# A two-headed sequence-mixer kernel (FFT convolution and diagonal state space): convolution rows split by parity, and its outer stages in pieces of the array

## The chip, the cores and the metric

The kernel runs on one core of one Trainium2 chip. The metric is device microseconds of one execution; lower is better. All tensors are bf16, sums are made in f32.

## The reference, cut to what matters

Two independent heads work on 2048 rows of 1024 channels and are written side by side.

```python
def _A_ref(q, k, v, shift_k, ssm_k, ssm_D):       # head A: (1, 2048, 1024)
    k_shift = zeros_like(k)
    for t in range(4):                            # a causal filter of 4 taps for each channel
        k_shift = k_shift + k_pad[:, t:t + S, :] * shift_k[:, 3 - t]
    kv = k_shift * v
    y = irfft2(rfft2(kv padded to 2S) * rfft2(ssm_k padded to 2S))[:S]   # a long convolution over rows
    return q * (y + kv * ssm_D)

def _B_ref(x, Lambda, Bmat, Cmat, log_dt, Dskip): # head B: 1024 complex states
    Lam_bar = exp(dt * Lam); Bu = x @ (((Lam_bar - 1) / Lam)[:, None] * Bmat).T
    for t in range(L): h = Lam_bar * h + Bu[t]    # a recurrence over the rows
    return 2 * (hseq @ Cmat.T).real + x * Dskip

return concatenate([a, b], axis=-1)               # (1, 2048, 2048)
```

## The kernel before, in words

Head A's convolution is a Fourier transform of length 4096 taken apart into two steps (128 by 32), in matrix products. Its rows are numbered n·16 + r, with n in 0..127 on the partitions and r in 0..15.

- **kv stage.** `kp` loads two rows r of k into the ring `kring`, `vp` two rows of v; `kvm`, `kva`, `kvb`, `kvc` (DVE) make kv. `am` (PE, L610) multiplies by the first Fourier matrix `F1t`, for two groups u of frequencies; `ae` (ACT) evicts, `ast` stores to the DRAM tile `Ys_kv`.
- **filter stage.** `hl` loads the filter `ssm_k` into `hk`, `hT` transposes on PE, `hm` (L643) is the same first step, `he` evicts, `hst` stores to `Ys_h`.
- **second step**, in 16 groups `gq`. `lh` and `lk` load 512 KiB each from `Ys_h` and `Ys_kv`; `sh`, `sk` (PE, L676) multiply by a table `wts`, in quarters of the array (64 by 64); `she`, `ske` (ACT) evict. For the complex product, `sw` copies the filter's result onto the neighbouring partitions by four DMAs of 128 KiB, so that real and imaginary parts are exchanged, and `pr` (DVE, L704) multiplies both. `sa` (PE, L717) goes back, `sae` evicts, `vst` stores to `Vs`.
- **last step.** `vl` loads from `Vs`, `a3` (PE, L744) multiplies by the last matrix `Gt`, `a3e` evicts, `qm` multiplies by q (loaded by `qp`), `ost` stores to the output.

Head B: `bl` loads and `bT` (PE, L458) transposes the matrix B, `bc` evicts it to `BT`; `cx` and `x` load C and x by DMA transposes. In 16 chunks of 128 rows: `U` (PE, L492), `ue`, `r1`..`r4` and `sc` (DVE; `sc` is a scan over the recurrence), `y` (PE, L546), `ye`, `yst`.

Everything is written out by hand: a long table, `ORDER`, gives the sequence of all these steps, which is the order on every engine, and behind each colon the buffers that the step takes. Transfers go on the queue of SP or POOL: `spd` on SP unless the word has `@G`, `gpd` on POOL unless it has `@S`. On each queue they are issued in this order, and a transfer that waits for a buffer or for data holds back those behind it.

In DRAM the rows of one transfer of 128 partitions are evenly spaced: `kr = k.rearrange("(n s) d -> n s d", s=NR)` for k, v, q and the output, and, for the 512 KiB loads and stores of the second step,

```python
    Ys_kv = tc.dram_tile([2, NR, P, D], BF16, name="Ys_kv")
    Ysv = lambda Y, gq: Y.rearrange("u r (e g) d -> (u r e) g d", g=32)[:, 2 * gq:2 * gq + 2, :]
```

Of the kernel before, what the change touches and what calls it, by code (L numbers as in the profile page):

```python
# [14 lines left out]
ALU = mybir.AluOpType  # L15
# [12 lines left out]
def a_constants():  # L28
    n1 = np.arange(64)[:, None]; k1 = np.arange(64)[None, :]
    ang = 2 * np.pi * n1 * (k1 + 0.5) / N1  # L30
    F = np.stack([np.cos(ang), -np.sin(ang)], axis=1).reshape(64, 2, 2, 32)
    F1 = np.zeros((64, 2, 2, 2, 2, 32))
    G1 = np.zeros((2, 2, 32, 2, 64, 2))
    for h in range(2):
        F1[:, h, :, h] = np.transpose(F, (0, 2, 1, 3))
        G1[h, :, :, :, :, h] = np.transpose(F, (1, 3, 2, 0)) * (2 / NFFT)
# [5 lines left out]
    WF = np.zeros((2, N2, 2, 32, 3, N2))  # L42
    t = lambda a: np.transpose(a, (0, 2, 1, 3))
    WF[:, :, 0, :, 0, :] = t(c_); WF[:, :, 1, :, 0, :] = t(s_)
    WF[:, :, 0, :, 1, :] = t(-s_); WF[:, :, 1, :, 1, :] = t(c_)
    WF[:, :, :, :, 2, :] = WF[:, :, :, :, 0, :]
    WI = np.zeros((2, 2, N2, 16, 2, 2, N2, 2))
    for gi in range(2):
        for ui in range(2):
            for gq in range(16):  # L50
                cc = np.transpose(c_[ui, 2 * gq + gi], (1, 0)); ss = np.transpose(s_[ui, 2 * gq + gi], (1, 0))
                o = WI[gi, :, :, gq, ui]
                o[0, :, 0, :, 0] = cc; o[0, :, 0, :, 1] = ss
                o[1, :, 0, :, 0] = -cc; o[1, :, 0, :, 1] = -ss
                for cp in range(2):
                    o[cp, :, 1, :, 0] = -ss; o[cp, :, 1, :, 1] = cc
    W = np.concatenate([WF.reshape(128, NWP, 4 * 96), WI.reshape(128, NWP, 2 * 256)], axis=2)
# [5 lines left out]
NA = 11  # L63
# [15 lines left out]
ue.2.1 ae.4.0:b13 hm.0.2.0:d2 am.4.1:d1 z2 ast.4.0 am.0.0:d0 U.2.3.0:p0 hst.0.1.1 ae.4.1:b4 U.1.1.1 he.0.2.0:b7 ast.4.1@S sc.0 U.2.3.1 ue.1.1
hst.0.2.0@S hm.0.2.1:d1 cx.7.1 ue.2.3 am.5.1:d2 ae.0.0:b6 hT.0.4:p1 cx.2.1 am.2.0:d0 hc.0.4:b10 ast.0.0 U.1.0.0:p0 ae.2.0:b3 hT.0.7:p1 cx.4.0 kva.8  # L80
U.1.0.1 ue.1.0 hT.0.5:p0 hc.0.7:b0 hl.5:a9 kvb.8:a4 hl.4:a2 U.2.0.0:p1 hc.0.5:b13 ast.2.0@S hl.7:a3 r3.0:m0 U.1.3.0:p0 he.0.2.1:b8 am.1.0:d0 hst.0.2.1
hm.0.5.0:d1 U.1.3.1 cm.0:a7 kvc.8 U.2.0.1 ue.1.3 he.0.5.0:b11 r4.0 U.4.0.0:p0 ue.2.0 hm.0.4.0:d1 r1.1:m0 U.4.0.1 he.0.4.0:b5 U.4.2.0:p1 ue.4.0:a5
hst.0.4.0@S ae.5.1:b6 hm.0.7.1:d1 r2.1 U.4.2.1 ae.1.0:b4 ast.5.1 U.4.1.0:p0 hl.6@G:a10 r1.2:m0 he.0.7.1:b7 ast.1.0@S hst.0.5.0 am.8.1:d2 ue.4.2
U.4.1.1 hm.0.5.1:d0 sc.1 am.5.0:d1 he.0.5.1:b8 U.4.3.0:p1 ue.4.1 am.2.1:d0 ae.5.0:b3 y.0.0.0:p0 ae.2.1:b13 hm.0.4.1:d1 hm.0.7.0:d0 ast.2.1@S U.4.3.1
x.3:b6 he.0.7.0:b10 r2.2:a0 am.8.0:d0 ae.8.1:b5 hst.0.7.0 y.0.0.1 r3.1:m0 hst.0.5.1 ue.4.3 ast.8.1@S ast.5.0@S y.0.0.2 ae.8.0:b0 vp.3:a8 y.0.1.0:p1
ast.8.0 cm.1 hst.0.7.1 r4.1 am.3.0:d2 y.0.1.1 ae.3.0:b4 r1.4:m0 y.0.0.3 ast.3.0 ye.0.0:b11 hT.1.4:p0 y.0.1.2 sc.2 hc.1.4:b13 he.0.4.1:b10 hT.1.3:p0
hm.1.4.1:d0 am.9.0:d2 hc.1.3:b9 hst.0.4.1@S ae.9.0:b8 hT.1.5:p0 am.9.1:d1 y.0.1.3 he.1.4.1:b5 r2.4:a5 am.3.1:d2 ye.0.1 hst.1.4.1 hm.1.3.1:d0
y.1.1.0:p1 he.1.3.1:b0 kvm.6:m0 hc.1.5:b3 y.1.1.1 hst.1.3.1@S ae.3.1:b7 hT.1.7:p0 y.1.1.2 ae.9.1:b4 hm.1.4.0:d0 hm.1.5.1:d2 hc.1.7:b10 ast.9.1 y.1.1.3
kp.6 kva.6 hT.1.6:p0 ast.9.0@S ye.1.1:b5 kp.5 hm.1.7.0:d1 hc.1.6:b13 yst.0@S y.1.0.0:p1 ast.3.1@S he.1.5.1:b0 hT.1.1:p0 cm.2:a4 kvb.6:a1 y.1.0.1
hst.1.5.1 hc.1.1:b4 lw.1@G:w0 hm.1.6.0:d2 r3.2:m0 y.1.0.2 he.1.6.0:b2 y.1.0.3 he.1.4.0:b8 hst.1.6.0@S hT.1.0:p0 r4.2 ye.1.0 hst.1.4.0 hm.1.6.1:d2  # L90
# [56 lines left out]
def full_kernel(ctx, tc, A_q, A_k, A_v, A_shift_k, A_ssm_k, A_ssm_D, B_x, B_Lre, B_Lim, B_Bre, B_Bim,  # L147
# [96 lines left out]
    def k8(name, shape):  # L244
        return rtile(ap_pool("a2"), "e", name, shape)
# [578 lines left out]
```

## Time and profile before

| | |
|---|---|
| median of three runs | 377.3 us (377.26, 377.30, 383.09) |
| the profiled execution | span 378.5 us |
| busy: PE, DVE, ACT, POOL | 346.6, 324.6, 264.2, 81.3 us |
| moved by DMA | 100.06 MB, mean 264 GB/s over the 16 DMA engines |

Times are microseconds unless marked ns. PE is the matrix engine, PEld its weight loads, DVE the vector engine, ACT the scalar engine, POOL GpSimd, SP the queue engine; a q behind a name is its sequencer. A row of a group gives line, engine, operation, what it writes and reads, and the count; then busy time and mean ns of one; then the idle time of the engine just before, and what ended it. In a row of a DMA queue stand packets, MB and the share of the 16 engines' time that these packets took.

### The profile page before, as it was taken

What the parts mean: (1) busy time and instruction counts of PE and PEld (TensorE: products, weight loads), DVE (VectorE), ACT (ScalarE), POOL (GpSimd) and SP (SyncE); (2) the same over time, 40 slices, a digit from 0 to 9 for tenths busy, and PEclk for the clock granted to TensorE, in tenths of its full rate; (3) what the DMA queues carried; (4) which work ended last, traced back from release to release, by engine and by line L of the source; (5) the groups of instructions that cost most, each with busy time, mean ns of one, the idle gap of its engine ahead of it and who ended that gap; (6) DMA issues with size and microseconds to landing.
All of it is one profiled execution on the core that took longest, in us unless ns stands there. A gap on an engine that the chain in (4) does not pass through costs nothing.

```text
span 378.5 us, 8748 instructions
## 1 busy us (share of the span) xinstructions
PE 346.6 (92%) x3661; PEld 225.6 (60%) x3661; DVE 324.6 (86%) x229; ACT 264.2 (70%) x341; POOL 81.3 (21%) x150
## 2 busy tenths in 40 slices
PE   4548889899899999999999999989999999999995
PEld 3226678785455578855444757367867664467442
DVE  6989599999999997999997797576899999993972
ACT  4978798877778886952785879778869771346433
POOL 7300023022112521214200325330210202211021
PEclk9999999999999999999999999999999999999999
DMA  6999999997578999999999897999989539877995
GB/s 231 317 338 216 265 272 286 296 314 235 200 243 270 247 313 287 281 272 268 190 275 312 258 324 234 220 267 221 284 236 312 175 125 325 306 229 255 350 319 206
DMA packets 67418, 100.06 MB, mean 264 GB/s; under 512 B 38435, under 2 KB 42147, under 8 KB 67380
## 3 DMA queue, kind: packets, MB, share of 16 engines
q1 hardware_dynamic: 54660, 56.32, 54.8%
q0 software_dynamic: 12720, 43.19, 36.8%
q8 instruction: 28, 0.46, 0.5%
q14 instruction: 10, 0.08, 0.1%
HBM read 49.16 MB, written 33.55 MB: 219 GB/s over the span
## 4 chain that ended last, share of the span: by engine, by line
PE 56%; DMA 15%; issue 13%; ACT 7%; SPq 4%; POOL 2%; DVE 1%; POOLq 0%; ACTq 0%; DVEq 0%
PE ps_u L492 22%; PE ps_y L546 16%; PE ps_a L744 4%; DMA wts<-a_c_W 4%; SPq L483 4%; DMA Ys_kv<-ysb 3%; PE ps_a L643 3%; DMA l2k<-Ys_kv 3%; DMA ld<-in_B_B_re_dram 3%; PE ps_a L717 3%; PE ps_a L610 3%; DMA hab<-hab 2%; PE ps_a L676 2%; PE ps_t L630 2%; ACT ysb L615 2%
## 5 line engine op out<-in xcount | busy, mean ns | idle before, releaser
L492 PEld LDWEIGHTS <-BT 128*128 128x128 bf16 x2048 | 119.3, 98 | 22.6 <-issue 11.7
L492 PE MATMUL ps_u<-xT,BT 128*128 128x128 bf16 x2048 | 127.7, 219 | 2.4 <-ACT u L497 1.2
L546 PE MATMUL ps_y<-CT,h 128*128 128x512 bf16 x512 | 127.7, 379 | 0.0
L546 PEld LDWEIGHTS <-h 128*128 128x128 bf16 x512 | 44.6, 98 | 48.0 <-issue 6.1
L523 DVE TENSOR_TENSOR_SCAN h<-rtab,h 128x2080 bf16<-128x2080 f32 x16 | 71.8, 4488 | 0.2
L497 ACT CAST u<-ps_u 128x512 bf16<-128x512 f32 x64 | 38.2, 603 | 27.0 <-PE ps_u L492 19.1
L506 DVE TENSOR_TENSOR mt<-u,Z 128x4096 bf16<-128x4096 bf16 x16 | 36.7, 2291 | 15.8 <-ACT u L497 15.4
L704 DVE TENSOR_TENSOR hab<-x,hab 128x4096 bf16<-128x4096 bf16 x16 | 36.5, 2286 | 15.2 <-DMA hab<-hab 10.5
L556 ACT CAST yo<-ps_y 128x512 bf16<-128x512 f32 x32 | 19.1, 596 | 28.0 <-PE ps_y L546 24.4
L650 ACT CAST ysbh<-ps_a 128x1024 bf16<-128x1024 f32 x32 | 32.3, 1033 | 8.8 <-PE ps_a L643 7.5
L691 ACT CAST x<-ps_a 128x1024 bf16<-128x1024 f32 x32 | 31.9, 1026 | 8.8 <-PE ps_a L676 5.9
L506 DVE TENSOR_TENSOR mt<-h,Z 128x4096 bf16<-128x4096 bf16 x16 | 36.7, 2292 | 0.5
L724 ACT CAST vsb<-ps_a 128x1024 bf16<-128x1024 f32 x32 | 31.7, 1027 | 6.5 <-PE ps_a L717 6.0
L583 DVE TENSOR_TENSOR mt<-kring,wbc 128x2048 bf16<-128x2048 bf16 (+3 forms) x14 | 35.8, 2592 | 0.4 <-ACT wbc L473 0.2
L615 ACT CAST ysb<-ps_a 128x1024 bf16<-128x1024 f32 x32 | 32.3, 1043 | 2.7 <-issue 1.6
L685 ACT CAST hab<-ps_a 128x1024 bf16<-128x1024 f32 x32 | 32.2, 1030 | 2.1 <-PE ps_a L676 1.9
L551 PE MATMUL ps_y<-Dd,xT 128*128 128x128 bf16 x128 | 28.0, 219 | 0.0
L749 ACT CAST ot<-ps_a 128x1024 bf16<-128x1024 f32 x16 | 15.7, 1018 | 14.1 <-PE ps_a L744 14.1
L169 POOL DMA_DIRECT2D Ys_h<-ysbh x20 | 14.3, 716 | 43.3 <-ACT ysbh L650 43.3
L168 POOL DMA_DIRECT2D hab<-hab x32 | 15.6, 494 | 32.1 <-ACT hab L685 18.3
L458 PE MATMUL ps_t<-ident,ld 128*128 128x128 bf16 x128 | 13.9, 285 | 9.1 <-DMA ld<-in_B_B_re_dram 4.4
L643 PE MATMUL ps_a<-hT,F1t 128*128 128x512 bf16 x64 | 20.6, 402 | 0.8 <-ACT ysbh L650 0.6
(116 smaller groups left out, 381.8 us busy)
## 6 DMA issues: line engine op xcount, KB each, us to landing
Ys_h<-ysbh POOLq DMA_DIRECT2D x20, 256.0 KB, 5.5
l2h<-Ys_h SPq DMA_DIRECT2D x9, 512.0 KB, 9.7
Vs<-vsb SPq DMA_DIRECT2D x9, 512.0 KB, 4.3
vv<-Vs SPq DMA_DIRECT2D x9, 512.0 KB, 5.2
Ys_kv<-ysb POOLq DMA_DIRECT2D x17, 256.0 KB, 6.2
l2k<-Ys_kv SPq DMA_DIRECT2D x8, 512.0 KB, 3.9
hab<-hab SPq DMA_DIRECT2D x32, 128.0 KB, 5.4
l2k<-Ys_kv POOLq DMA_DIRECT2D x8, 512.0 KB, 7.8
```

Source lines behind the costliest of these rows:

```text
L492: nc.tensor.matmul(pu[:, w, jl, :], BT[:, 2 * jp + jl, w, d, :], xT[:, d, :], start=(d == 0), stop=(d == ND - 1))
L497: nc.scalar.copy(u[:, :, 2 * jp:2 * jp + 2, :], st["pu", i, jp][:])
L506: nc.vector.tensor_mul(m, s_, w_)
L523: nc.vector.tensor_tensor_scan(gf, rtab[:].rearrange("p a j t -> p (a j t)"), gf, 0.0, ALU.mult, ALU.add)
L546: nc.tensor.matmul(py[:], h[:, 1 - w, j, 2:TP], CT[:, j, w, dh * 512:(dh + 1) * 512], start=(j == 0 and w == 0), stop=(j == NJ - 1 and w = ...
L583: nc.vector.tensor_mul(m[:, :, j0:j0 + n, :], a_, wbc[:, j0:j0 + n, :].unsqueeze(1).to_broadcast([P, 2, n, DV]))
L615: nc.scalar.copy(st["ysb", r, u][:], st["pa", r, u][:].rearrange("p e d -> p (e d)"))
L643: nc.tensor.matmul(pd[:, e, :], F1t[:, u, :], st["hT", f, rp][:, e, :], start=True, stop=not sk)
L650: nc.scalar.copy(st["yh", f, rp, u][:], st["pa", f, rp, u][:])
L685: nc.scalar.copy(hab[:, a, :, e * 512:(e + 1) * 512], st["ps", key, gq, e][:])
L691: nc.scalar.copy(x16[:, :, e * 512:(e + 1) * 512], st["ps", "k", gq, e][:])
L704: nc.vector.tensor_mul(hab, x16.unsqueeze(1).to_broadcast([P, 2, 2 * D]), hab)
```

## The change

It rewrites head A's data layout and half of B's load. Its parts:

1. **Rows by parity.** Row numbers are read as (n, h, s): h is the parity of the block of 16 rows. The partition is now h·64 + n. A load of k, v, q and a store of head A's output takes both parities in one transfer, whose DRAM side has the counts [2][64][2048] (output [2][64][1024]) in place of [128][2048].
2. **Outer stages in array pieces.** `am` works on parities and frequency groups in quarters of the array (64 by 64); `a3` has 64 output rows for each parity, in halves. The DRAM tiles are `[NR, 2, P, D]`, one store `ast` for both halves, and the second step's loads and stores have the counts [4][32][2048] in DRAM.
3. **Real and imaginary on one partition.** `sh`, `sk` and `sa` run in eighths of the array (64 by 32, and 32 by 64), with real and imaginary parts beside each other in the free dimension. The 64 copies `sw` and `pr` go; `p1` multiplies with the parts read in the other order, `p0` without.
4. **Filter rows in C's space.** `hk` is two tiles of 16 KiB per partition, one after the other in the place that the second half of C (`ct`) takes later. So the second filter load, on POOL, waits for the first half's transposes `hT`, and the loads of C's second half, on SP from `cx.7.1` on, wait for the second half's.
5. **Half of B by DMA transpose**: `bx` loads 8 of the 16 tiles straight into `BT`; their `bl`, `bT`, `bc` go.
6. Small: `dd` is one DVE product, not 8 ACT copies; `sc` is two scans of 1040 in place of one of 2080, on one table; the order and the buffers are all new.

| transfer | KiB | on SP, on POOL before | on SP, on POOL now | DRAM counts now |
|---|---|---|---|---|
| k (r ≥ 0) | 512 | 3, 5 | 8, 0 | 2, 64, 2048 |
| v | 512 | 4, 4 | 6, 2 | 2, 64, 2048 |
| q | 512 | 6, 2 | 4, 4 | 2, 64, 2048 |
| output of A | 256 | 9, 7 | 10, 6 | 2, 64, 1024 |
| l2h | 512 | 9, 7 | 10, 6 | 4, 32, 2048 |
| l2k | 512 | 8, 8 | 12, 4 | 4, 32, 2048 |
| Vs | 512 | 9, 7 | 11, 5 | 4, 32, 2048 |
| hab copies | 128 | 32, 32 | none | |

```diff
-    Ys_kv = tc.dram_tile([2, NR, P, D], BF16, name="Ys_kv")
+    Ys_kv = tc.dram_tile([NR, 2, P, D], BF16, name="Ys_kv")
...
-    kr = k.rearrange("(n s) d -> n s d", s=NR)
-    oar = out_a.rearrange("(n s) d -> n s d", s=NR)
+    rows = lambda a: a.rearrange("(n h s) d -> h n s d", s=NR, h=2)
+    two = lambda a, r: a.rearrange("(n h s) d -> h n (s d)", s=NR, h=2)[:, :, 2 * r * D:(2 * r + 2) * D]
+    flat = lambda t_: t_.rearrange("p s d -> p (s d)")
+    oar = rows(out_a)
...
-    Ysv = lambda Y, gq: Y.rearrange("u r (e g) d -> (u r e) g d", g=32)[:, 2 * gq:2 * gq + 2, :]
+    Ysv = lambda Y, gq: Y.rearrange("r h (e g) d -> e (r h) (g d)", g=32)[:, :, 2 * gq * D:(2 * gq + 2) * D]
...
-            spd(t_, kr[:, 2 * r:2 * r + 2, DX:])
+            spd(flat(t_), two(k, r))
...
-        spd(st["v", r][:], vr[:, 2 * r:2 * r + 2, :])
+        spd(flat(st["v", r][:]), two(v, r))
...
-            nc.tensor.matmul(pd[:, e, :], F1t[:, u, :], kvt(r)[:, r % 2, e * 512:(e + 1) * 512], start=True, stop=True)
+            for h in range(2):
+                for u in range(2):
+                    nc.tensor.matmul(st["pa", r][e][64 * u:64 * u + 64, h, :], F1t[64 * h:64 * h + 64, 2, 64 * u:64 * u + 64],
+                                     kvt(r)[64 * h:64 * h + 64, r % 2, e * 512:(e + 1) * 512], start=True, stop=True,
+                                     tile_position=(64 * h, 64 * u))
...
-    def sw(gq):
-        hab = st["hab", gq]
-        for b in range(4):
-            o = b ^ 1
-            spd(hab[32 * b:32 * b + 32, 1, :, :], hab[32 * o:32 * o + 32, 0, :, :])
-        nc.vector.tensor_mul(hab, x16.unsqueeze(1).to_broadcast([P, 2, 2 * D]), hab)
+    def p1(gq):
+        nc.vector.tensor_mul(st["pq", gq][:], st["sk", gq][:], st["sh", gq][:, :, ::-1, :])
+    def p0(gq):
+        nc.vector.tensor_mul(st["sh", gq][:], st["sk", gq][:], st["sh", gq][:])
...
+        for ri in range(2):
+            for j in range(4):
+                for u in range(2):
+                    nc.tensor.matmul(pd[u][32 * j:32 * j + 32, ri, :], wt[up, b0:b0 + 32],
+                                     st[nm, gq][up, j // 2, (j % 2) * 512:(j % 2 + 1) * 512], start=True, stop=True,
+                                     tile_position=(64 * u, 32 * j))
...
-            for u in range(2):
-                nc.tensor.matmul(pd[:, e, :], Gt[:, u, :], st["vv", r][:, u, e * 512:(e + 1) * 512], start=(u == 0), stop=(u == 1))
+            for h in range(2):
+                nc.tensor.matmul(pd[64 * h:64 * h + 64, e, :], Gt[:], st["vv", r][:, h, e * 512:(e + 1) * 512], start=True, stop=True,
+                                 tile_position=(0, 64 * h))
...
-        spd(st["qt", r][:], qr[:, 2 * r:2 * r + 2, :])
+        spd(flat(st["qt", r][:]), two(q, r))
...
-    E["ost"] = lambda r: gpd(oar[:, r, :], st["ot", r][:])
+    E["ost"] = lambda r: gpd(oar[:, :, r, :], st["ot", r][:])
```

Three places on SP's queue show how the transfers stand. The rows give line, operation, what is written and read, and the counts of the written side. The first place is near the start, where k, the filter and the first x are loaded; before:

```order
L168 DMA hk<-in_A_ssm_k_dram 128x2048
L168 DMA ld<-in_B_B_re_dram 128x1024
L168 DMA kring<-in_A_k_dram 128x2048
L483 DMA_TRANSPOSE xT<-in_B_x_dram 128x8x128
L480 DMA_TRANSPOSE CT<-in_B_C_im_dram 128x8x128
```

and now, from the first k load with both parities:

```order
L155 DMA kring<-in_A_k_dram 128x1x2048
L155 DMA hk<-in_A_ssm_k_dram 128x2048 x4
L460 DMA_TRANSPOSE BT<-in_B_B_im_dram 128x8x128
L155 DMA ld<-in_B_B_re_dram 128x1024
L460 DMA_TRANSPOSE BT<-in_B_B_re_dram 128x8x128
L155 DMA kring<-in_A_k_dram 128x1x2048
L463 DMA_TRANSPOSE ct<-in_B_C_re_dram 128x8x128
L155 DMA v<-in_A_v_dram 128x1x2048
```

All eight k loads are now on SP, with four filter loads and the B transposes between them; the written side of a k load stays 128 partitions, in three counts like its source. The second place is the second step, where loads of l2h and l2k, stores of Vs and, before, the copies within `hab` alternate; before:

```order
L168 DMA l2k<-Ys_kv 128x2048
L168 DMA hab<-hab 32x2048 x4
L169 DMA out_dram<-yo 128x1024
L483 DMA_TRANSPOSE xT<-in_B_x_dram 128x8x128
L168 DMA l2h<-Ys_h 128x2048
L483 DMA_TRANSPOSE xT<-in_B_x_dram 128x8x128
L169 DMA Vs<-vsb 128x2048
```

and now:

```order
L155 DMA l2k<-Ys_kv 128x1x2048 x3
L155 DMA l2h<-Ys_h 128x1x2048
L468 DMA_TRANSPOSE xT<-in_B_x_dram 128x8x128
L156 DMA Vs<-vsb 4x32x2048
L155 DMA l2k<-Ys_kv 128x1x2048 x2
L156 DMA Vs<-vsb 4x32x2048
```

The copies are gone, more of the loads follow each other on SP, and the store to Vs has the counts 4, 32, 2048. The third place is SP's end, with the last loads of q and Vs and the stores of both heads (`ot` is head A's, `yo` head B's); before:

```order
L168 DMA qt<-in_A_q_dram 128x2048
L169 DMA out_dram<-ot 128x1024 x4
L169 DMA out_dram<-yo 128x1024
L169 DMA out_dram<-ot 128x1024
L169 DMA out_dram<-yo 128x1024
```

and now:

```order
L155 DMA qt<-in_A_q_dram 128x1x2048
L155 DMA vv<-Vs 128x2x1024 x3
L156 DMA out_dram<-ot 2x64x1024 x3
L156 DMA out_dram<-yo 128x1024
L156 DMA out_dram<-ot 2x64x1024 x6
L156 DMA out_dram<-yo 128x1024
L156 DMA out_dram<-ot 2x64x1024
```

The loads of q all stand ahead of the last stores, ten of head A's stores end SP's queue, and each has the counts 2, 64, 1024.

More of the change, by code (lines that the diff above doesn't have):

```diff
@@ L666, in full_kernel, with s2 @@
     E["lk"] = lambda gq: l2("l2k", Ys_kv, gq)
[L668 removed]
+    def s2(key, nm, gq):
         wt = st["w", gq // 2]
[L670 to L678 removed]
@@ new lines, in full_kernel, with spe @@
+    E["sh"] = lambda gq: s2("h", "l2h", gq)
+    E["sk"] = lambda gq: s2("k", "l2k", gq)
+    def spe(key, gq, u):
+        s16 = once(("s" + key, gq), lambda: k4("s16", [P, 2, 2, 512]))
+        nc.scalar.copy(s16[:, u, :, :], st["ps", key, gq][u][:])
+    E["she"] = lambda gq, u: spe("h", gq, u)
+    E["ske"] = lambda gq, u: spe("k", gq, u)
+    def p1(gq):
+        st["pq", gq] = k4("pq", [P, 2, 2, 512])
+        nc.vector.tensor_mul(st["pq", gq][:], st["sk", gq][:], st["sh", gq][:, :, ::-1, :])
@@ new lines, in full_kernel, with sa @@
+    E["p1"] = p1
+    def p0(gq):
+        nc.vector.tensor_mul(st["sh", gq][:], st["sk", gq][:], st["sh", gq][:])
+    E["p0"] = p0
+    def sa(gq):
+        wt = st["w", gq // 2]
+        pd = [dtile("ps_a") for _ in range(2)]
+        st["ps", "v", gq] = pd
+        for t, (m, src, ri) in enumerate(((0, "sh", 0), (1, "sh", 1), (2, "pq", 0), (2, "pq", 1))):
+            for j in range(4):
+                for u in range(2):
+                    jp = slice(32 * j, 32 * j + 32)
+                    b0 = 256 + (gq % 2) * 384 + u * 192 + m * 64
+                    nc.tensor.matmul(pd[j // 2][64 * u:64 * u + 64, j % 2, :], wt[jp, b0:b0 + 64],
+                                     st[src, gq][jp, u, ri, :], start=(t == 0), stop=(t == 3),
+                                     tile_position=(32 * j, 64 * u))
```

357 lines of the change are left out of this document (154 added, 203 removed).

## The prediction

> **What bounds the kernel now.** I read the page's head first, then the slices, the chain, and the kernel by stages.
>
> ```profile
> span 378.5 us, 8748 instructions
> PE 346.6 (92%) x3661; PEld 225.6 (60%) x3661; DVE 324.6 (86%) x229; ACT 264.2 (70%) x341; POOL 81.3 (21%) x150
> ...
> PE   4548889899899999999999999989999999999995
> DMA  6999999997578999999999897999989539877995
> GB/s 231 317 338 216 265 272 286 296 314 235 200 243 270 247 313 287 281 272 268 190 275 312 258 324 234 220 267 221 284 236 312 175 125 325 306 229 255 350 319 206
> DMA packets 67418, 100.06 MB, mean 264 GB/s; under 512 B 38435, under 2 KB 42147, under 8 KB 67380
> ...
> q1 hardware_dynamic: 54660, 56.32, 54.8%
> q0 software_dynamic: 12720, 43.19, 36.8%
> ...
> PE 56%; DMA 15%; issue 13%; ACT 7%; SPq 4%; POOL 2%; DVE 1%; POOLq 0%; ACTq 0%; DVEq 0%
> 0.00:20.00 20.00, 9.48 (x55) 5.66 (x56) 16.40 (x50) 14.26 (x23) 10.56 (x25) 1.00 0.87 273
> 20.00:40.00 20.00, 13.77 (x84) 8.73 (x84) 17.79 (x21) 14.57 (x28) 1.27 (x2) 1.00 1.12 279
> ```
>
> PE is busy 92% of the span, and leads the chain with 56%. Of its idle 32 us, the first 40 us hold 40 − 9.48 − 13.77 = 16.8 us. After that PE is the bound, DVE close behind. But the second resource is as full as PE: the packets took 54.8% + 36.8% = 91.6% of the time of all 16 DMA engines. That holds because every large transfer is even over the 16; whatever puts more on a few of them makes these the bound. The profiled execution (378.5 us) is 0.3% over the median of the runs (377.3), so I make the sums against the span and give them as times.
>
> **The transfers, the term that decides.** What sets how many engines a transfer uses? Nearly all of the kernel's have 128 rows on both sides. The small parameter loads near the start do not:
>
> ```profile
> praw<-in_B_log_dt_dram SPq DMA_DIRECT2D x1, 2.0 KB
> praw<-in_B_Lambda_re_dram SPq DMA_DIRECT2D x1, 2.0 KB
> praw<-in_B_Lambda_im_dram SPq DMA_DIRECT2D x1, 2.0 KB
> praw<-in_B_Dskip_dram SPq DMA_DIRECT2D x1, 2.0 KB
> ...
> q1 hardware_dynamic: 64, 0.01, 2.2%
> ```
>
> The last row is of the window 1.6 to 3.8 us, when SP's queue moved just these four: 64 packets, 0.01 MB. Four loads of 8 rows make 32 data packets, so 32 others are completions: 8 a load, not 16. A transfer whose outer count is 8 went to 8 engines, one share and one completion each. The change gives outer counts of 2 (k, v, q, output) and 4 (l2h, l2k, Vs) on the DRAM side. If a transfer is cut along its outermost count, these go to 2 and to 4 engines.
>
> The Trainium skill says so: in "DMA: Bandwidth & Descriptors", section "Why a DMA increments its semaphore by 16 and not by 1", the engines are the largest number up to 16 that divides the outermost count of both sides, on SP's queue the lowest-numbered ones, on GpSimd's a run of neighbours from a cursor that moves on. By that, 128 against 2 gives 2 engines, always the same pair on SP. The trace agrees for 8 rows (the 64 packets); no run here shows a count that differs between the sides, or which engines serve.
>
> Whether SP's share always falls on the same pair no row tells; I take it so, since nothing in the program would move it, and keep the other case as a rival. Bytes on each engine of that pair, from the table of the change:
>
> - SP, count 2: k, v, q are 18 × 524,288 B, A's output 10 × 262,144 B: 12.06 MB, halved 6.03 MB.
> - SP, count 4: 33 × 524,288 B = 17.30 MB, a quarter 4.33 MB.
> - POOL, counts 2 and 4: 21 × 524,288 + 6 × 262,144 B = 12.58 MB; evenly spread 0.79 MB.
> - All else: 100.06 MB, less 64 copies of 131,072 B (8.39), plus 0.25 for the longer tables, is 91.92; less the three sums above it is 49.98 MB, a sixteenth 3.12 MB.
>
> Together 14.27 MB on each of two engines, against 100.06 / 16 = 6.25 MB now. Their rate:
>
> ```profile
> DMA packets 287, 0.86 MB, mean 430 GB/s; under 512 B 32, under 2 KB 32, under 8 KB 286
> ```
>
> That is the window 350 to 352 us, one of the fastest: 430 / 16 = 26.9 GB/s an engine. The best slice of the page has 350 / 16 = 21.9, the mean 264 / 16 = 16.5. The 10.36 MB of confined transfers are rows of 2 to 4 KB like that window's: 10.36 / 26.9 = 385 us. The other 3.91 MB have small packets among them; SP's queue moved 56.32 MB in 54.8% of 16 × 378.5 us, 17.0 GB/s: 230 us. Sum **615 us** in which the pair must work. Not all overlaps: two stage joins leave it waiting.
>
> ```profile
> Ys_kv<-ysb POOLq DMA_DIRECT2D x17, 256.0 KB, 6.2
> Vs<-vsb SPq DMA_DIRECT2D x9, 512.0 KB, 4.3
> vv<-Vs SPq DMA_DIRECT2D x9, 512.0 KB, 5.2
> out_dram<-ot SPq DMA_DIRECT2D x9, 256.0 KB, 5.0
> ```
>
> Between the last k and the first l2k stand a store (6.2) and about 12 us of kv work (an estimate from the DVE and ACT groups of that stage); between the last Vs and the outputs 4.3 + 5.2 us and about 2.5 of PE and ACT; at the end 5.0. That is 35 us: **650 us**. The ends: everything at 26.9 GB/s, 14.27 / 26.9 = 530 us; everything at 16.5, 865 us.
>
> What waits there: a k load that now needs 262,144 / 26.9 GB/s = 9.7 us of its pair holds `kvm`, and the transposes of B, x and C behind it on the same engines complete only with their last share; so `U` on PE waits too. The removed copies and PE work give nothing back while PE waits for loads.
>
> **The other parts**, which decide only if the transfers spread:
>
> ```profile
> L492 PE MATMUL ps_u<-xT,BT 128*128 128x128 bf16 x2048 | 127.7, 219 | 2.4 <-ACT u L497 1.2 <-ACT BT L473 0.9 <-ACT hT L635 0.3
> L458 PE MATMUL ps_t<-ident,ld 128*128 128x128 bf16 x128 | 13.9, 285 | 9.1 <-DMA ld<-in_B_B_re_dram 4.4 <-DMA ld<-in_B_B_im_dram 2.5 <-ACT BT L473 1.2
> L610 PE MATMUL ps_a<-acc,F1t 128*128 128x512 bf16 x64 | 19.0, 387 | 0.4 <-ACT ysb L615 0.2 <-ACT ysbh L650 0.2
> L676 PE MATMUL ps_a<-l2h,wts 64*64 64x512 bf16 x128 | 11.3, 387 | 3.0 <-DMA wts<-a_c_W 2.3 <-DMA l2h<-Ys_h 0.7
> L676 PE MATMUL ps_a<-l2k,wts 64*64 64x512 bf16 x128 | 10.8, 385 | 0.0
> L717 PE MATMUL ps_a<-hab,wts 64*64 64x512 bf16 x256 | 18.2, 383 | 0.8 <-DVE hab L704 0.7
> L744 PE MATMUL ps_a<-vv,Gt 128*128 128x512 bf16 x64 | 16.1, 379 | 0.0
> L473 ACT COPY BT<-ps_t 128x1024 bf16<-128x1024 bf16 x14 | 13.9, 1013 | 4.9 <-PE ps_t L458 4.9
> L704 DVE TENSOR_TENSOR hab<-x,hab 128x4096 bf16<-128x4096 bf16 x16 | 36.5, 2286 | 15.2 <-DMA hab<-hab 10.5 <-ACT x L691 4.6
> L518 DVE TENSOR_TENSOR h<-mt 128x2048 bf16<-128x2048 bf16 x16 | 19.5, 1220 | 0.3
> L523 DVE TENSOR_TENSOR_SCAN h<-rtab,h 128x2080 bf16<-128x2080 f32 x16 | 71.8, 4488 | 0.2
> ```
>
> - PE, B: 64 of 128 transposes go, half of 13.9: −7.0 us; 8 evictions of 1.013 go from ACT, under PE's work.
> - PE, `am`: 64 products at 19.0 us become 128 in quarters; at L717's 18.2 / 256 = 71 ns that is 9.1: −9.9.
> - PE, `a3`: 64 of half the array. Between half of 16.1 us (two beside each other, as the quarters run four) and all of it; I take half: −8.0.
> - PE, second step: 512 quarters at 11.3 + 10.8 + 18.2 = 40.3 us become 1024 eighths. If eight run beside each other, 40.3; if each costs what a quarter does (71 ns), 72.7; if as L492's pairs of load and product (127.7 / 2048 = 62 ns), 63.5. Ends 0 and +32; I take +10, nearer the quarters, which already ran four at once.
> - DVE: 16 products at 2.286 become 32 at 1.220: +2.5. Halving the length from 4096 to 2048 costs 2 × 1.220 − 2.286 = 0.15 us an extra instruction, so 16 more scans cost 2.4. `dd` on DVE is one product of 1024, below the 1.220 of a 2048 one. DVE ends 15.2 us of waits at L704, 10.5 of them for the copies; that is more than the added 6, and PE covers both.
> - The wait on the filter's place (part 4): behind `cx.7.1` on SP stand the other C loads and x. It waits for a transpose written just ahead of it in the table; at no more than 2 to 3 us it hides under the 16.8 us of PE's early idleness; uncovered, it adds itself.
> - The added price of issuing is none: 64 issues fewer.
>
> Sum on PE: −7.0 − 9.9 − 8.0 + 10 = −15, ends −25 and +15 (with `a3` at no gain and eighths at quarters' price).
>
> On the eighths the Trainium skill ("TensorE: Matmul & The Clock Gate", "Packing small matmuls — row/col tiling") has pieces in different places of the array start about 4 ns apart and run together; by that the step stays near 40 us and the sum is −25. The trace shows four at once, 71 ns where L744's full products take 16.1 / 64 = 252 ns; no run here shows eight.
>
> **The rivals.**
>
> 1. *The transfers spread over all 16 engines* (the cut is made on the 128 partitions, or across both counts). For it: the SBUF side still has 128; the row for 8 rows had 8 on both sides, so it can't tell. Then PE decides: 378 − 15 = **362 us**, ends 353 and 393. This is the side that is not slower; the point is the number of engines: 16 in place of 2.
> 2. *Spread, and the small pieces cost their issue*: the same with +32 and no gain at `a3`: **393 us**.
> 3. *Few engines at a time, but not the same ones each time.* Total load falls to 91.92 / 16 = 5.75 MB an engine, less than now. Single transfers last 9.7 us in place of the 4 to 6 us of the landings above; those on the way between stages show: two joins and the first k, about 5 us each: 362 + 15 = **377 us**.
> 4. *Only one of the counts confines.* With 2 spread: 4.33 MB at 26.9 and about 4.7 at 17: 435 us. With 4 spread: 6.03 and about 5.0: 518 us.
>
> **How the numbers follow.** The confined case 0.79, predicted 650 us, its own range 530 to 865; rival 4 gets 0.04, rival 1 0.11, rival 3 0.04, rival 2 0.02. The range reaches down to 430 to take in rival 4 and up to 865: about 0.81 inside. Within 2% (370 to 385 us; 2% is about what a measurement of this kernel can tell from no change) lies rival 3 and a bit of rival 1: 0.05. Faster 0.10, slower 0.85.
>
> **What would show it.** Right: landings of k, v and q rise from about 5 to well over 15 us and those of transposes with them, mean GB/s falls to about 92 MB / 650 us = 141 while the slices of DMA never show more than two or three tenths for long, PE busy near half, and the chain is DMA by most of its share. Wrong in the step on counts: landings stay near 5 us and the mean over 240 GB/s. Wrong in the rate: few engines, but a span far from 650, by waits of SP at its own queue. If the pieces of the array mislead, it is seen in the busy time of `sh`, `sk` and `sa`, against 40.3 us.

## The result, and the profile after

The changed kernel takes **702.5 us** (median of four executions, 701.4 to 704.4), the kernel before 377.3 beside it on the same chip: the ratio is 1.865, 95% interval 1.856 to 1.874. The forecast was 650, in the range 430 to 865. The executions of some of the kernels below scatter by 1 to 2% on a chip, and one of run 7 took 1936 us; each ratio and interval leaves the disturbed ones out, while the medians given take all.

The page of the kernel after, its head, slices, queues and chain; the profiled execution took 704.4 us.

```profile
span 702.4 us, 9560 instructions
PE 375.7 (53%) x4133; PEld 232.9 (33%) x4173; DVE 321.2 (46%) x258; ACT 259.0 (37%) x329; POOL 58.8 (8%) x92
...
PE   4762048045477498995859575656068600392300
...
DMA  8998964299979959955543337122355224464111
GB/s 212 156 113 64 90 157 180 99 90 150 134 143 264 105 201 88 160 188 96 70 127 110 128 131 215 54 118 117 118 172 182 78 95 140 155 216 136 72 62 53
DMA packets 85881, 92.03 MB, mean 131 GB/s; under 512 B 58671, under 2 KB 64319, under 8 KB 85840
...
q1 hardware_dynamic: 62768, 58.76, 50.0%
q0 software_dynamic: 23072, 32.67, 15.0%
...
DMA 43%; PE 20%; SPq 20%; issue 7%; ACT 4%; DVE 1%; POOL 0%; POOLq 0%; ACTq 0%
```

No engine is the bound any more: PE is busy 53%, and the two queues' packets took 65% of the engines' time where it was 91.6%. Bytes fell by 8%, but the rate halved from 264 to 131 GB/s. Read the two DMA rows together at the right end. In the last slices one tenth of the 16 engines moves 62 and 53 GB/s: two engines at the 26.9 GB/s of the prediction make 53.8. That is what two engines look like in this view.

What waits, by group and by landing of transfers on POOL's queue (for SP's confined transfers the page gives no landing). "Confined" is used below for a transfer whose small outer count keeps it on a few engines. Before, then after:

```profile
L583 DVE TENSOR_TENSOR mt<-kring,wbc 128x2048 bf16<-128x2048 bf16 (+3 forms) x14 | 35.8, 2592 | 0.4 <-ACT wbc L473 0.2
...
qt<-in_A_q_dram POOLq DMA_DIRECT2D x2, 512.0 KB, 4.5
...
v<-in_A_v_dram POOLq DMA_DIRECT2D x4, 512.0 KB, 5.4
```

```profile
L571 DVE TENSOR_TENSOR mt<-kring,wbc 128x2048 bf16<-128x2048 bf16 (+3 forms) x14 | 36.1, 2594 | 83.7 <-DMA kring<-in_A_k_dram 83.6
...
L727 PE MATMUL ps_a<-vv,Gt 128*64 128x512 bf16 x64 | 10.7, 447 | 53.0 <-DMA vv<-Vs 52.3
...
Vs<-vsb POOLq DMA_DIRECT2D x5, 512.0 KB, 14.2
...
qt<-in_A_q_dram POOLq DMA_DIRECT2D x4, 512.0 KB, 28.6
...
v<-in_A_v_dram POOLq DMA_DIRECT2D x2, 512.0 KB, 18.3
```

DVE's first kv product waited 83.6 us for k and PE 52.3 us for Vs, where the same groups before (L583, L744) had 0.4 and 0.0 us of idle time in all. And from SP's timeline, its three longest transposes of B:

```profile
20.76 13.15 SPq L460 DMA_TRANSPOSE BT<-in_B_B_im_dram  x1
...
47.49 11.66 SPq L460 DMA_TRANSPOSE BT<-in_B_B_re_dram  x1
59.84 10.26 SPq L460 DMA_TRANSPOSE BT<-in_B_B_re_dram  x1
```

The longest issues of a transpose before were 8.41 us (of x, at 12.71 us) and 6.70. SP stands still while it issues, and everything behind it on its queue waits too. It is not the transposes alone: the plain stores of head A's output, before and after (duration of one issue, least, median and most, in ns):

```profile
L169 SPq DMA_DIRECT2D out_dram<-ot x9: 332/350/919, 343.7 to 372.2; - x9
```

```profile
L156 SPq DMA_DIRECT2D out_dram<-ot x10: 512/4190/13132, 626.9 to 687.4; - x10
```

Added up over the trace, SP stood at the issue of transposes for 185 us (82 before) and of plain transfers for 242 us (78 before). In the chain, the three lines of transposes (L460, L463, L468) are 14 of the 20% of SPq.

### The profile page after: what moved, and what is told of

It reads as the page before. It is cut to its first block, busy times and chain, and to the rows that moved or that the text cites. A ratio compares the mean times of both kernels' runs of the same rounds, so it can differ in the third digit from the quotient of the medians.

```text
span 702.4 us, 9560 instructions
## 1 busy us (share of the span) xinstructions
PE 375.7 (53%) x4133; PEld 232.9 (33%) x4173; DVE 321.2 (46%) x258; ACT 259.0 (37%) x329; POOL 58.8 (8%) x92
## 4 chain that ended last, share of the span: by engine, by line
DMA 43%; PE 20%; SPq 20%; issue 7%; ACT 4%; DVE 1%; POOL 0%; POOLq 0%; ACTq 0%
DMA l2k<-Ys_kv 10%; PE ps_u L477 8%; SPq L460 7%; PE ps_y L532 6%; DMA wts<-a_c_W 5%; DMA Vs<-vsb 5%; DMA Ys_h<-ysbh 5%; DMA xT<-in_B_x_dram 5%; DMA l2h<-Ys_h 4%; SPq L463 4%; SPq L468 4%; DMA v<-in_A_v_dram 4%; SPq L156 3%; DMA vv<-Vs 3%; SPq L155 3%
## 5 line engine op out<-in xcount | busy, mean ns | idle before, releaser
L477 PE MATMUL ps_u<-xT,BT 128*128 128x128 bf16 x2048 | 140.4, 233 | 65.9 <-DMA BT<-in_B_B_im_dram 32.4
L477 PEld LDWEIGHTS <-BT 128*128 128x128 bf16 x2048 | 132.6, 106 | 86.7 <-issue 41.4
L532 PE MATMUL ps_y<-ct,h 128*128 128x512 bf16 x483 | 134.7, 409 | 19.3 <-ACT yo L542 12.8
L678 ACT CAST s<-ps_a 128x1024 bf16<-128x1024 f32 x64 | 61.4, 1021 | 97.2 <-PE ps_a L670 86.5
L571 DVE TENSOR_TENSOR mt<-kring,wbc 128x2048 bf16<-128x2048 bf16 (+3 forms) x14 | 36.1, 2594 | 83.7 <-DMA kring<-in_A_k_dram 83.6
L509 DVE TENSOR_TENSOR_SCAN h<-rtab,h 128x1040 bf16<-128x1040 f32 x32 | 72.5, 2306 | 0.0
L684 DVE TENSOR_TENSOR pq<-s,s 128x2048 bf16<-128x2048 bf16 x16 | 19.6, 1224 | 105.7 <-ACT s L678 72.6
L737 DVE TENSOR_TENSOR ot<-ot,qt 128x1024 bf16<-128x1024 bf16 x16 | 10.5, 689 | 97.9 <-ACT ot L733 97.7
L643 ACT CAST ysbh<-ps_a 128x1024 bf16<-128x1024 f32 x32 | 32.2, 1040 | 43.5 <-DMA Ys_h<-ysbh 36.3
L733 ACT CAST ot<-ps_a 128x1024 bf16<-128x1024 f32 x16 | 15.6, 1021 | 80.1 <-PE ps_a L727 64.2
L727 PE MATMUL ps_a<-vv,Gt 128*64 128x512 bf16 x64 | 10.7, 447 | 53.0 <-DMA vv<-Vs 52.3
L670 PE MATMUL ps_a<-l2h,wts 64*32 64x512 bf16 x256 | 12.5, 448 | 44.3 <-DMA l2h<-Ys_h 23.2
L670 PE MATMUL ps_a<-l2k,wts 64*32 64x512 bf16 x256 | 13.1, 469 | 37.2 <-DMA l2k<-Ys_kv 34.8
## 6 DMA issues: line engine op xcount, KB each, us to landing
Ys_kv<-ysb POOLq DMA_DIRECT2D x8, 512.0 KB, 10.4
```

The lines of the kernel that those rows point to most:

```text
L477: nc.tensor.matmul(pu[:, w, jl, :], BT[:, 2 * jp + jl, w, d, :], xT[:, d, :], start=(d == 0), stop=(d == ND - 1))
L509: nc.vector.tensor_tensor_scan(gf, rtab[:].rearrange("p j t -> p (j t)"), gf, 0.0, ALU.mult, ALU.add)
L532: nc.tensor.matmul(py[:], h[:, 1 - w, j, 2:TP], st["CT", dh][:, j, w, :], start=(j == 0 and w == 0), stop=(j == NJ - 1 and w == 1))
L571: nc.vector.tensor_mul(m[:, :, j0:j0 + n, :], a_, wbc[:, j0:j0 + n, :].unsqueeze(1).to_broadcast([P, 2, n, DV]))
L643: nc.scalar.copy(st["yh", f, rp, u][:], st["pa", f, rp, u][:])
L670: nc.tensor.matmul(pd[u][32 * j:32 * j + 32, ri, :], wt[up, b0:b0 + 32], st[nm, gq][up, j // 2, (j % 2) * 512:(j % 2 + 1) * 512], start=Tr ...
```

## The experiments

**1 to 3: the confined transfers made whole.** The change, with its transfers of count 2 cut into two of 64 partitions, those of count 4 into four of 32, so that each one's outer count is 64 or 32 on both sides. First all of them, then only those of count 2, then only those of count 4.

```diff
-            spd(flat(t_), two(k, r))
+            for h in range(2):
+                spd(flat(t_)[64 * h:64 * h + 64, :], two(k, r)[h])
...
-        spd(st[nm, gq][:], Ysv(Ys, gq))
+        for e in range(4):
+            spd(flat(st[nm, gq][:])[32 * e:32 * e + 32, :], Ysv(Ys, gq)[e])
```

> The changed kernel with every transfer of outer count 2 sent as two of 64 partitions, and every one of outer count 4 as four of 32 partitions, so that the outermost count is 64 or 32 on both sides; same queues, same order, nothing else. Theory (few engines): the engines of a transfer are as many as its outermost count allows, so all 16 serve again, and the time falls from 702 us to the sum of the other parts, 353 to 393 us, near 365; 127 more issues on the queues cost little. Rival (the array pieces, the lower granted clock of PE or the new order are slow by themselves): the time stays above 600 us.

> Only the transfers of outer count 2 (k, v, q, head A's output) are halved; those of count 4 stay. Theory: the loaded engines are four with 17.30 / 4 = 4.33 MB of SP's confined transfers and about 4.7 MB of all else, 161 + 274 = 435 us of work, with the waits that the full change showed about 470 to 510 us. Rival (the slowness lies in something else): no change from 702 us, or all of the gain if count 4 confines nothing, 365 us.

> Only the transfers of outer count 4 (l2h, l2k, Vs) are sent as four of 32 partitions; those of count 2 stay. Theory: two engines with 6.03 MB of SP's confined transfers and about 5.0 MB of all else, 225 + 293 = 518 us of work, with waits about 540 to 590 us. Rival (count 2 confines nothing): 365 us.

Measured: all whole **400.8 us** (ratio to before 1.054, 1.043 to 1.065), only count 2 whole **518.0** (two executions, 512.7 and 523.3), only count 4 whole **600.0** (1.583, 1.563 to 1.603). The two single ones lie above what was expected of them (470 to 510 and 540 to 590). (The 127 more issues of the first expectation are SP's alone; POOL has 57 more.) The same bytes and the same work on the engines, 302 us less: the outer counts are what slowed the kernel. The page of the first, and its landings on POOL's queue for q and v (28.6 and 18.3 us above):

```profile
span 401.8 us, 9882 instructions
PE 343.1 (85%) x4133; PEld 219.3 (55%) x4173; DVE 320.2 (80%) x258; ACT 257.9 (64%) x329; POOL 80.3 (20%) x149
...
DMA packets 75793, 92.02 MB, mean 229 GB/s; under 512 B 48579, under 2 KB 54227, under 8 KB 75748
...
qt<-in_A_q_dram POOLq DMA_DIRECT2D x8, 256.0 KB, 8.7
...
v<-in_A_v_dram POOLq DMA_DIRECT2D x4, 256.0 KB, 5.1
```

The trace's packet records show the few engines directly. How long exactly two, or exactly four, packets of 1 KB and more were open on SP's queue:

| kernel | exactly two, us | exactly four, us |
|---|---|---|
| before | 12 | 8 |
| all whole | 8 | 7 |
| only count 4 confined (second run) | 26 | 150 |
| only count 2 confined (third run) | 211 | 6 |
| both (the change) | 229 | 153 |

The records don't name the engines, but SP's transfers seem to share the same ones: after its last issue, at 687.9 us, the change still had 0.75 MB of its 256 KB stores to move, almost three of them, and mostly one or two packets were open at a time on that queue, 57 GB/s to the end.

The sizes can be estimated from bytes alone. SP's count 2 puts 6.03 MB on each of its pair instead of an even 12.06 / 16 = 0.75, so 5.28 MB more, at 26.9 GB/s 196 us. SP's count 4 puts 4.33 instead of 1.08 MB: 3.25 MB, 121 us. Measured:

| confined | us more than all whole | from bytes |
|---|---|---|
| count 4 only (second run) | 117 | 121 |
| count 2 only (third run) | 199 | 196 |
| both (the change) | 302 | 317 |

The pair's surplus adds to the whole time almost one for one, as if nothing overlapped it. Two cautions: all whole pays for its cuts, some 25 us by run 6, which the change doesn't; and SP's held issues grew with the surplus too (209 us in all whole, 230, 402 and 427 in the three rows). The runs don't separate the pair's own work from what SP's held queue adds.

**4: the confined transfers on POOL's queue.** The change with every transfer of count 2 and 4 issued by POOL; nothing else.

```diff
-            spd(flat(t_), two(k, r))
+            nc.gpsimd.dma_start(flat(t_), two(k, r))
```

> All transfers of counts 2 and 4 are issued by POOL, single as in the change; the rest stays where it is. Theory that SP's confined transfers fall on the same engines each time while POOL's move on: each engine has 91.9 / 16 = 5.75 MB, a single transfer still takes 5 to 10 us of its engines, and the time falls far below 702 us, to 400 to 520 us, held up by POOL's queue, where all of them stand in one line. Rival (the engines are the same on both queues): the first two then carry 6.3 + 2.1 + 6.3 MB of confined transfers and about 2.9 MB of all else, 17.6 MB, so 700 to 900 us.

Measured: **563.9 us** (1.488, 1.471 to 1.505), between the two cases and 139 less than the change. Were POOL's always the same pair, all 16.8 MB of count 2 and 25.2 MB of count 4 would give each of the pair 8.4 + 6.3 = 14.7 MB, where SP's share in the change is 10.4; the kernel would be slower than the change, and it is faster. So POOL's engines are not one fixed pair. The Trainium skill has them move on ("DMA: Bandwidth & Descriptors", section "Why a DMA increments its semaphore by 16 and not by 1"); the run agrees so far, and its packet records do: exactly 12 packets of 1 KB and more were open on POOL's queue for 38 us (9 in the kernel before), as with three transfers of four engines each. It doesn't make confined transfers cheap. With no pair loaded above the others the surplus rule gives nothing over all whole, and 163 us came; the landings rose instead:

```profile
kring<-in_A_k_dram POOLq DMA_DIRECT2D x8, 512.0 KB, 23.2
v<-in_A_v_dram POOLq DMA_DIRECT2D x8, 512.0 KB, 20.6
...
BT<-in_B_B_im_dram SPq DMA_TRANSPOSE x4, 15.9
```

**5: the count alone, in the kernel before.** Only its loads of k, v and q get the counts [2][64][2048].

```diff
-            spd(t_, kr[:, 2 * r:2 * r + 2, DX:])
+            spd(flat(t_), two(k, r))
```

> The kernel before, and only the loads of k (r >= 0), v and q made with the counts [2][64][2048] on the DRAM side (they fetch other rows, so the output is not the reference's; bytes, instructions and order stay). On SP are 3 + 4 + 6 = 13 of these 24 loads. Theory, an outer count of 2 confines a load to 2 engines, on SP always the same: each of the pair gets 13 x 524,288 / 2 = 3.41 MB at 26.9 GB/s, 127 us, and 93.3 MB / 16 = 5.83 MB at 17.0 GB/s, 343 us: 470 us, range 410 to 500. Rival, it is another part of the change that slows the kernel: 377 us, at most 385.

Measured: **511.7 us** (1.350, 1.336 to 1.364). The mechanism needs nothing else of the change. It is above the range: by the surplus rule of the first runs, (3.41 − 0.43) MB / 26.9 GB/s = 111 us on top of 381.1 would be 492, and 131 came. The waits at k, v and q are those of the changed kernel again:

```profile
DVE mt L585 <- DMA kring<-in_A_k_dram: 44.0, 4, 21.9
...
DVE acc L606 <- DMA v<-in_A_v_dram: 36.7, 3, 22.0
DVE ot L755 <- DMA qt<-in_A_q_dram: 34.7, 3, 15.8
```

**6: the price of cutting.** All whole took 400.8, not the 362 forecast for transfers that spread. The first suspect is the cut itself: the same cuts in the kernel before.

```diff
-            spd(t_, kr[:, 2 * r:2 * r + 2, DX:])
+            for h in range(2):
+                spd(t_[64 * h:64 * h + 64, :, :], kr[64 * h:64 * h + 64, 2 * r:2 * r + 2, DX:])
```

> The kernel before, and only its large transfers cut as in the run of the change with all of them whole: k, v, q and A's output as two transfers of 64 partitions, l2h, l2k and Vs as four of 32; 184 more issues, the same bytes. It separates why that run took 401 us rather than the forecast 362. Theory 1, the added issues (SP and POOL held longer, shorter transfers) cost it: 390 to 400 us here. Theory 2, the price lies in the change's own order and layout (its first 100 us): here 377 to 381.

Measured: **406.1 us** (1.059, 1.042 to 1.076): cutting alone costs 25 us. Where? The first 80 us of the kernel before and of this one, as span, then PE, PEld, DVE, ACT, POOL busy, granted clock, DMA share, GB/s:

```profile
0.00:80.00 80.00, 59.41 (x650) 45.67 (x651) 69.40 (x89) 61.69 (x91) 18.31 (x38) 1.00 1.07 275
```

```profile
0.00:80.00 80.00, 40.84 (x436) 31.59 (x443) 62.99 (x83) 49.74 (x76) 18.66 (x40) 0.92 1.06 220
```

PE has done 18.6 us less work by then, at the same DMA share but 220 instead of 275 GB/s. That this is most of the 25 us is not shown: in run 8 PE is 19.3 us behind at the same point, and the kernel loses 8. SP's timeline and ACT's waits show one stall. SP stood 16.5 us at the issue of two DMA transposes of C, and at the same time ACT waited for a store of the filter that had been issued just before them:

```profile
59.53 16.53 SPq L480 DMA_TRANSPOSE CT<-in_B_C_im_dram  x2
```

```profile
ACT ysbh L652 <- DMA Ys_h<-ysbh: 16.8, 1, 16.8
```

**7: eighths of the array, in the kernel before.** `sh` and `sk` as 512 products of 64 by 32 in place of 256 of 64 by 64.

```diff
-                nc.tensor.matmul(pd[64 * gi:64 * gi + 64, u, :], wt[up, b0:b0 + 64],
...
+                for ri in range(2):
...
+                    nc.tensor.matmul(pd[c0:c0 + 32, u, :], wt[up, b0:b0 + 32],
```

> The kernel before, and only sh and sk in eighths of the array (64 by 32): 512 products where 256 quarters were, the same result. If eight run beside each other, their busy time stays near 11.3 + 10.8 = 22.1 us and the kernel within 1%. If each costs what a quarter does, it becomes 44 us and the kernel about 20 us longer, 397. The run of the change with whole transfers had 23 us for the two, so I expect 22 to 25 us and 377 to 381.

Measured: 382.3 us beside 381.1 (1.006, 0.998 to 1.013). The two groups:

```profile
L678 PE MATMUL ps_a<-l2h,wts 64*32 64x512 bf16 x256 | 11.5, 383 | 1.5 <-DMA l2h<-Ys_h 1.0 <-DMA wts<-a_c_W 0.5
L678 PE MATMUL ps_a<-l2k,wts 64*32 64x512 bf16 x256 | 11.0, 382 | 0.0
```

22.5 us for 512 eighths where 256 quarters took 22.1: twice the pieces at almost no price, so eight run beside each other.

**8: half of B by DMA transposes, in the kernel before.** `bl`, `bT`, `bc` of tiles 0 to 3 become `bx` at the place of `bl`.

```diff
-ld_par bl.4.0@G:b0 bl.5.0@G:b1 bl.5.1@G:b2 bl.4.1:b3 bl.6.0:b4 bl.2.1@G:b5 ld_sd@S bl.1.1@G:b6
+ld_par bl.4.0@G:b0 bl.5.0@G:b1 bl.5.1@G:b2 bl.4.1:b3 bl.6.0:b4 bx.2.1 ld_sd@S bx.1.1
```

> The kernel before, and only 8 of the 16 tiles of B (rows 0 to 3) loaded by DMA transposes on SP in place of load, PE transposes and eviction. Theory, PE's 7 us and ACT's 8 are saved and the DMA transposes cost nothing that shows: 370 to 374 us. Rival, the transposes are the price in the run of the change with whole transfers (PE waited there for BT): SP is held at their issue and 64 more small-packet transposes crowd the engines in the first 100 us: 380 to 395 us.

Measured: **389.3 us** (1.025, 1.014 to 1.037): 8 us slower, with 64 of PE's 128 transposes less. Its first 80 us:

```profile
0.00:80.00 80.00, 40.15 (x414) 30.50 (x421) 54.05 (x80) 45.91 (x72) 17.54 (x34) 0.94 1.06 225
```

Again the share stays and the rate falls, from 275 to 225 GB/s.

**9 and 10: which cuts cost.** Run 6 in two halves: only k and v cut (16 more issues), and only the rest (168 more).

```diff
+            for h in range(2):
+                spd(st["v", r][64 * h:64 * h + 64, :, :], vr[64 * h:64 * h + 64, 2 * r:2 * r + 2, :])
```

> The kernel before, and only the loads of k (r >= 0) and v cut into two transfers of 64 partitions: 16 more issues. Cutting all the large transfers (184 more issues) cost 25 us, 406.1 against 381.1. Theory 1, the price is per issue, 25 / 184 = 0.14 us: here 2 us, 383. Theory 2, it is paid in the first 80 us, where SP stood 16.5 us at the issue of two DMA transposes of C while k, v and the filter's stores moved: here 395 to 400.

> The complement of the run with k and v cut: the kernel before, and only q and A's output cut into two transfers and l2h, l2k, Vs into four, 168 more issues, none of them in the first 80 us. Theory 1 (per issue): 23 us, 404. Theory 2 (the first 80 us): 383 to 388.

Measured: k and v cut 389.3 us (1.025, 1.002 to 1.048), the rest cut 391.4 (1.033, 0.995 to 1.072), beside 379.6. The medians lie between the two theories: 16 more issues, 9 of them in the first 80 us, go with about 10 us, and 168 later ones with about 12. But the intervals reach from under 1 to 18 us and from −2 to 27 us, so neither theory is ruled out, nor is it shown whether the price is that of issues or of smaller transfers.

**11: `am` in quarters alone, without any count of 4.** An attempt at a version that beats both.

```diff
-            nc.tensor.matmul(pd[:, e, :], F1t[:, u, :], kvt(r)[:, r % 2, e * 512:(e + 1) * 512], start=True, stop=True)
+                o = 64 * (h ^ u)
+                nc.tensor.matmul(pd[o:o + 64, u, :], F1t[64 * h:64 * h + 64, 2, 64 * u:64 * u + 64],
+                                 kvt(r)[64 * h:64 * h + 64, r % 2, e * 512:(e + 1) * 512], start=True, stop=True,
+                                 tile_position=(64 * h, o))
```

> The kernel before, and of the change only am in quarters of the array, with k and v by parity in two transfers of 64 partitions each. The quarters lie crosswise (parity h to the column half h for the first group of frequencies, 1 - h for the second), so that a row of Ys_kv keeps 128 even partitions and l2h, l2k, Vs, q and the output stay whole transfers of 128 rows as before; its stores are of 1 KB rows. am's 19.0 us on PE should become 9 to 10.5. If PE's work decides, 381 - 9 plus the price of the cut k and v loads: 374 if that price is 2 us, 388 if it is 16.

Measured: 386.9 us (1.027, 1.004 to 1.051). `am` fell from 19.0 to 13.3 us, less than in the change (10.4 with all whole), while the cut loads of k and v had cost 9.7 in run 9. It beats neither the kernel before nor, beyond the scatter, run 9.

**12: all whole, and B loaded plainly.** Run 1 with `bx` taken back.

```diff
-U.1.0.0:p0 bx.6.1 sin1 bl.3.0:b5 par_rest U.1.0.1 bx.6.0
+U.1.0.0:p0 bl.6.1:b0 sin1 bl.3.0:b5 par_rest U.1.0.1 bl.6.0:b13
```

> The change with all of its large transfers whole (two of 64 partitions, four of 32), and the 8 tiles of B that it loads by DMA transposes loaded plainly again, transposed on PE and evicted by ACT, in the first 120 us. With the transposes that version took 400.8 us. If their price (8.3 us in the kernel before, 389.3 against 381.1) stands here too: 390 to 395, although PE and ACT have 7 and 8 us more work. Rival, PE's 7 us come back and nothing else: 400 to 408. Below 377 it would beat the kernel before; I don't expect that.

Measured: **409.0 us** (1.083, 1.074 to 1.091), 8 more than run 1. It came out nearest the rival (400 to 408): taking the DMA transposes of B back costs 8 us in the change's order, and putting them in cost 8 us in the order of the kernel before. So what such a part is worth depends on the order around it; what in the order decides was not tested. No version tried beats the kernel before.

## Why the prediction was right, and where it was off

- **The step on counts: right.** Runs 1 and 5 show it from both sides, one by taking the counts away, one by adding them alone, and the packet records show two and four packets open for 229 and 153 us. That SP's transfers fall on the same engines each time, which no row told beforehand, is supported by the end of SP's queue, where almost three stores went mostly one or two packets at a time, and by run 4, where POOL's do not.
- **The rate of the pair, 26.9 GB/s: right.** Two engines moved 53 GB/s in the last slice. The table of runs 1 to 3 gives 121, 196 and 317 us from it against 117, 199 and 302.
- **The size, 52 us short, is in the base.** The prediction had 333 us beside the surplus (650 − 317): the pair's even share by bytes, and 35 us for "Not all overlaps: two stage joins leave it waiting". All whole it is 400.8: 68 more, less the 15 by which the two surpluses fall short of 317. In runs 1 to 3 what the surplus adds to is the whole time of the kernel with its waits, not the pair's other bytes. Rival 4, worked out in the same way, was short too: 435 and 518 stood there, 518 and 600 came. The closeness of the size is in part luck: the same rule is 20 us short in run 5 and gives nothing of the 163 us of run 4, and the range, 430 to 865, was wide.
- **"Slices of DMA never show more than two or three tenths for long": wrong in the first half.** They show 8 and 9 there, at a low rate. The window 50 to 100 us of the kernel after has it (columns as above):

```profile
50.00:100.00 50.00, 9.57 (x101) 7.55 (x101) 24.24 (x17) 9.95 (x13) 0.57 (x2) 0.59 1.21 99
...
650.00:700.00 50.00, 6.30 (x34) 2.42 (x32) 3.37 (x5) 5.89 (x7) 1.41 (x2) 0.60 0.17 64
```

  All 16 engines count as busy at 99 GB/s, because packets of the transposes are open on them: packets of 256 bytes are 802 of the 967 us of engine time there (more below). Only in the tail, where no transposes are left, the view is as forecast.
- **Landings, rate, PE, chain:** over 15 us for q and v on POOL (28.6 and 18.3), 141 GB/s (131), near half (53%): right. For k and the transposes the page has no landings; in run 4 k's were 23.2 us. The chain was to be DMA by most of its share, and has DMA 43% and SPq 20%; that SP itself would be held was named only as a way to be wrong.
- **The other parts, from the groups of run 1:**

```profile
L673 PE MATMUL ps_a<-l2k,wts 64*32 64x512 bf16 x256 | 11.9, 381 | 0.5 <-DMA l2k<-Ys_kv 0.5
...
L703 PE MATMUL ps_a<-s,wts 32*64 32x512 bf16 x256 | 11.9, 387 | 1.9 <-ACT vsb L710 1.5 <-DVE s L691 0.2 <-PE ps_a L703 0.2
...
L673 PE MATMUL ps_a<-l2h,wts 64*32 64x512 bf16 x256 | 11.5, 396 | 6.5 <-DMA wts<-a_c_W 5.1 <-DMA l2h<-Ys_h 1.4
...
L703 PE MATMUL ps_a<-pq,wts 32*64 32x512 bf16 x256 | 11.5, 386 | 0.0
...
L601 PE MATMUL ps_a<-acc,F1t 64*64 64x512 bf16 x128 | 10.4, 389 | 1.0 <-ACT ysb L608 0.5 <-ACT ysbh L645 0.4
...
L734 PE MATMUL ps_a<-vv,Gt 128*64 128x512 bf16 x64 | 8.8, 386 | 2.4 <-DMA vv<-Vs 1.8 <-ACT ot L740 0.7
...
L439 PE MATMUL ps_t<-ident,ld 128*128 128x128 bf16 x64 | 7.7, 300 | 6.8 <-DMA ld<-in_B_B_im_dram 5.8 <-DMA ld<-in_B_B_re_dram 1.0
```

  `am` −8.6 (forecast −9.9), `a3` −7.3 (−8.0), the transposes of B −6.2 (−7.0), the second step 46.8 against 40.3, +6.5 (+10): together −15.6, forecast −15. The scan rose by 0.7, not 2.4. The groups were sized rightly, but their sum is not PE's time: groups overlap (before, they add up to 413 us where PE is busy 346.6), and PE's busy time fell by 3.5 us only, to 343.1, at a mean granted clock of 0.953 against 1.000. Its idle time went from 31.9 to 58.7 us (both are rough here, since 40 of 4173 products have no record). Of the 39 us between 362 and 400.8, run 6 accounts for about 25, the cut that this version needs and the change does not, if it costs the same in this order. The 12 us by which PE's busy time fell short of the groups' sum would be most of the rest, an estimate; run 12 speaks against the transposes of B as its cause. (378 − 15 is 363, not the 362 of rivals 1 and 3; nothing hangs on it.)
- **"The added price of issuing is none"**: right in the count, since the change issues less, but not in the time: SP stood at its issues for 427 us where it was 160 before.

## What to carry to other kernels

Before two rows of DRAM are joined into one transfer, look at its outermost count: with 2 there, a transfer of 512 KiB ran on two engines, and on SP's queue what these got above an even share, divided by 26.9 GB/s, added to this kernel's time nearly one for one (131 us for 111 in run 5). Cutting it instead has its price too (25 us in run 6, for 184 more issues), so here a layout whose 128 rows are evenly spaced on both sides was worth more than the PE time that another order of the rows saved. Before adding up such savings from groups, look whether the groups overlap. Read DMA share and GB/s together: high share with a low rate, or one tenth at 54 GB/s, pointed here at a few engines that others wait for.

## What the runs showed of the hardware

**DMA transposes suffer when a few engines are backlogged.** From the trace's packet records, the 256-byte packets, all but 32 of them of transposes (32,800 in the kernel before and in the last row, 40,992 in the others):

| kernel | mean ns | longest us | engine us in all |
|---|---|---|---|
| before | 30 | 2.2 | 969 |
| all whole | 28 | 2.1 | 1151 |
| only count 4 confined | 35 | 10.6 | 1437 |
| only count 2 confined | 76 | 11.3 | 3118 |
| after | 83 | 11.0 | 3383 |
| all confined on POOL | 60 | 6.8 | 2459 |
| before with k, v, q at count 2 | 60 | 13.3 | 1980 |

The median is 18 ns in all of them: a few packets stand open for microseconds. The stretch of 50 to 100 us, 16 engines busy at 99 GB/s, is made of these. That a transpose's packets on the other engines wait for its share on the backlogged ones would explain it; the runs show the association with the confined counts, not the way it works.

**SP is held at its issues while a few engines are backlogged.** Its issues took 160 us before, 209 all whole, 427 after; the median plain store of head A's output 0.35 us before and 4.19 after. Why SP is held, no run tells.

**PE's granted clock was low where PE was idle.** Its mean was 0.773 in the kernel after, at 53% busy. By stretches of 50 us of that kernel it was 1.00 at 47.8 us busy, 0.80 at 29.3 and 0.59 at 9.6 (the stretch of 50 to 100 us above). It is no rule of the busy share alone: the first 20 us before had 1.00 at 9.5 of 20 us busy. Busy times grow at the lower clock: the group of `sk` took 13.1 us after and 11.9 all whole, at 0.953.
